# Opening loads split over two DMA queues, the first tile and the last output tile worked in halves

## The chip, the cores and the metric

The kernel runs on one core of one Trainium2 chip. The metric is device time in microseconds (us) of one execution; lower is better. A core has a matrix engine (TensorE, PE in the profile), a vector engine (VectorE, DVE), a scalar engine (ScalarE, ACT), GpSimd (POOL) and SyncE (SP), which here only issues DMA transfers. Each works through its own list of instructions in order and waits on semaphores for the others. The DMA engines, 16 for the core, move data between DRAM and the on-chip memory; a queue of requests can belong to SP or to ACT. PSUM, where PE writes its results, has eight banks of 128 x 512 float32.

## The reference

The input x has 2048 rows (tokens) of 1024 columns. Two kinds of layer alternate, A, B, A, B, each added to x after a norm of every row:

```python
x = x + _A_ref(_layernorm(x), A_wqkv, A_wo)
x = x + _B_ref(_layernorm(x), B_w_gate, B_w_up, B_w_down)
# and the same two again
# _A_ref, 32 heads of 32 columns, with phi(t) = where(t > 0, t + 1, exp(t)) + 1e-6:
q, k, v = split(x @ wqkv)
kv, z = sum_s phi(k)[s] v[s]^T, sum_s phi(k)[s]
out = (phi(q) @ kv) / (phi(q) . z + 1e-6) @ wo
# _B_ref:
out = ((x @ w_gate) * (x @ w_up)) @ w_down
```

The values are bfloat16. The four norms all run over complete rows, so nothing of a tile can be normed before all its 1024 columns are there.

## The kernel before

The tokens are cut into 16 tiles of 128 rows, four tiles to a group. The tensor X holds all of them on the chip from beginning to end. The instructions of each engine stand in the order in which the code emits them; nothing is reordered, and the code places work of other engines between matmuls through small plans (`at(step, ...)`, `mid`). Buffers are taken from and returned to lists in turn (`slots` for 128 x 4096 buffers, `banks` for PSUM).

**Start.** All loads go through SP's queue in one file: tiles x0 and x1 (`load_x`, L93, 256 KB each), the first slab of key weights in two transfers (`load_cols` with `parts=2`, L99, 512 KB each: the first holds the weight rows for k = 0 to 3, the second those for k = 4 to 7), x2, x3, the second key slab (1 MB), x4, a value slab, and so on. A slab is the 1024 x 512 block of `wqkv` that makes 512 output columns. ACT begins with a load of its function table (L103). Transfers use eight semaphores in turn, so from the ninth on a request waits until the transfer eight before it has landed.

Meanwhile PE runs 11 matmuls on a zeroed buffer (`warm_up`, L125). For tile 0, `ln_stats` (L234, two halves of 512 columns, and L237) takes mean and variance on DVE, `ln_norm` computes the reciprocal deviation on ACT (L258, L260) and writes the normed tile `xn` on DVE (L262), and `tr_tile` has PE transpose it in eight 128 x 128 blocks into one PSUM bank (L279), which ACT copies out in two halves (L280, L281). Four more warm-up matmuls stand behind the transposes. The first group alone is transposed in this way; later groups are transposed by DMA requests in SP's list (L274).

Then `kv_eight` makes keys and values in chunks of one tile by 512 columns, eight matmuls over k to a chunk (L642). The first four chunks are (tile 0, slab 0), (tile 1, slab 0), (tile 0, slab 1), (tile 1, slab 1). The work for tiles 1, 2 and 3 is emitted between the matmuls of these chunks:

```python
order[0:4] = [(0, 0), (1, 0), (0, 1), (1, 1)]
mid.update({(0, 0, 5): ((tr_tile, 0, 1), (ln_norm, 0, 2), (ln_stats, 0, 3, (1,))),
            (1, 0, 5): ((ln_norm, 0, 3),),
            (0, 1, 3): ((tr_tile, 0, 2),), (1, 1, 3): ((tr_tile, 0, 3),)})
```

So the first chunk's six matmuls for k = 0 to 5 are followed by tile 1's transposes, then by k = 6 and 7.

**End.** The last step of the last layer (`down_seven` with `final`, i = 4) adds a product of 14 matmuls (L1182) to the PSUM bank of each of four tiles. For tiles 0 to 3 in turn: 14 matmuls of 128 x 512, then `after` has DVE scale the bank, add X and write X (`read`, L1155), and `finish` requests the store of that 128 x 512 block to `out` from SP (L1065, 128 KB).

Of the kernel before, what the change touches and what calls it, by code (L numbers as in the profile page):

```python
# [10 lines left out]
ALU = mybir.AluOpType  # L11
AX = mybir.AxisListType
BF16 = mybir.dt.bfloat16
# [22 lines left out]
def kernel(  # L36
# [11 lines left out]
    nc = tc.nc  # L48
    P = 128
    S, D = A_x.shape[1], A_x.shape[2]  # L50
    F = B_w_gate.shape[1]
    NT = S // P
    KD = D // P
    KH = KD // 2
# [3 lines left out]
    TPG = G // P  # L58
    NB = 512
    DC = D // NB  # L60
    NQD = KF // 2
    WPC = 7
# [10 lines left out]
    x_view = A_x[0].rearrange("(t p) d -> p t d", p=P)  # L73
    o_view = out[0].rearrange("(t p) d -> p t d", p=P)
    wqkv_v = A_wqkv.rearrange("(k p) n -> p k n", p=P)
# [5 lines left out]
    X = const.tile([P, NT, D], BF16, tag="X", name="X")  # L81
    slots = Free([const.tile([P, 4096], BF16, tag=f"s{i}", name=f"s{i}") for i in range(17)])
    temps = Free([const.tile([P, NB], F32, tag=f"f{i}", name=f"f{i}") for i in range(12)])
    banks = Free([psum.tile([P, NB], F32, tag=f"b{i}", name=f"b{i}") for i in range(8)])

    def v3(s, n):
        return s[:].rearrange("p (k n) -> p k n", n=n)

    def h3(s, n):
        return s[:].bitcast(F16).rearrange("p (k n) -> p k n", n=n)  # L90

    def load_x(t):
        nc.sync.dma_start(out=X[:, t, :], in_=x_view[:, t, :])  # L93

    def load_cols(view, n, parts=1):
        s = slots.get()
        w = KD // parts
        for r in range(parts):
            nc.sync.dma_start(out=v3(s, NB)[:, r * w:(r + 1) * w, :],  # L99
                              in_=view[:, r * w:(r + 1) * w, n * NB:(n + 1) * NB])  # L100
        return s

    nc.scalar.preload_act_table_set("natural_log_exp_and_others")  # L103
    wA = {}
    load_x(0)
    load_x(1)
    wA["k"] = [load_cols(wqkv_v, DC, 2)]
    load_x(2)
    load_x(3)
    wA["k"].append(load_cols(wqkv_v, DC + 1))  # L110
    load_x(4)
    wA["v"] = [load_cols(wqkv_v, 2 * DC)]
    load_x(5)
    load_x(6)
# [8 lines left out]
    def warm_up(n):  # L123
        for _ in range(n):
            nc.tensor.matmul(out=warmb[:], lhsT=warm[:].bitcast(BF16)[:, 0:P], rhs=warm[:].bitcast(BF16)[:, 0:NB],  # L125
                             start=True, stop=True)

    warm_up(11)
    ident = const.tile([P, P], BF16, tag="ident", name="ident")
# [121 lines left out]
        nc.scalar.activation(out=xn[:], in_=X[:, t, :], func=ACT.Identity, bias=nmr[:], scale=rstd[:])  # L251
        lns[(li, t)] = xn

    def ln_norm(li, t):
        mv = lns[(li, t)]
        half = li % 2 == 1
        rstd = small.tile([P, 1], F32, tag="rstd", name="rstd")
        nc.scalar.activation(out=rstd[:], in_=mv[:, 1:2], func=ACT.Ln, bias=(eps5x if half else eps5)[:],  # L258
                             scale=1.0 / (XS * XS) if half else 1.0)
        nc.scalar.activation(out=rstd[:], in_=rstd[:], func=ACT.Exp, scale=-0.5)  # L260
        xn = xnp.tile([P, D], F16 if li else BF16, tag="xn", name="xn")
        nc.vector.tensor_scalar(out=xn[:], in0=X[:, t, :], scalar1=mv[:, 0:1], scalar2=rstd[:],  # L262
                                op0=ALU.subtract, op1=ALU.mult)
        lns[(li, t)] = xn

    def tr_tile(li, t):
        xn = lns.pop((li, t))
        g, tl = divmod(t, TPG)
        if (li, g) not in xnTs:
            xnTs[(li, g)] = slots.get()  # L270
        s = xnTs[(li, g)]
        xnT = (h3 if li else v3)(s, NB)
        if (li, g) != (0, 0):
            nc.sync.dma_start_transpose(out=xnT[:, :, tl * P:(tl + 1) * P], in_=xn[:])  # L274
            return
        b = banks.get()
        pt = b[:].bitcast(BF16).rearrange("p (k n) -> p k n", n=P)
        for k in range(KD):
            nc.tensor.transpose(out=pt[:, k, :], in_=xn[:, k * P:(k + 1) * P], identity=ident[:])  # L279
        nc.scalar.copy(out=xnT[:, 0:KH, tl * P:(tl + 1) * P], in_=pt[:, 0:KH])  # L280
        nc.scalar.copy(out=xnT[:, KH:KD, tl * P:(tl + 1) * P], in_=pt[:, KH:KD])  # L281
        banks.put(b)

    def phi_exp(b, c):
        m = temps.get()
# [205 lines left out]
    def kv_seven(kvp):  # L491
# [5 lines left out]
        for t, i in zip(range(2 * TPG, NT), (3, 8, 17, 31, 36, 45, 59, 64)):  # L497
            at(i, ln_stats, 2, t, (0,))
            if i % 14 == 8:
                at(i + 5, ln_norm, 2, t)  # L500
                at(i + 6, tr_tile, 2, t)
            else:
                at(i + 4, ln_rstd, 2, t)
                at(i + 6, ln_apply, 2, t)
                at(i + 7, tr_tile, 2, t)
# [367 lines left out]
    def ffn_pass(li, p, W):  # L873
        q = li - 1 + p
        xs = [xnTs.pop((li, 2 * p + g)) for g in range(2)] + xqs.pop((li, p))
        x0, x1, ta, tb = (h3(s, NB) for s in xs)
        mv = [x0[:, 0:KH], x0[:, KH:KD], x1[:, KH:KD], tb[:, KH:KD], ta[:, 0:KH], ta[:, KH:KD], tb[:, 0:KH]]
        st = [0, 1, 7, 3, 4, 5, 6]
        hs = []
        wd = []  # L880
# [177 lines left out]
        def xrow(g, tl, n):  # L1058
            t = (2 * p + g) * TPG + tl
            return t, X[:, t, n * NB:(n + 1) * NB], o_view[:, t, n * NB:(n + 1) * NB]  # L1060

        def finish(g, tl, n):
            _, o, d = xrow(g, tl, n)
            if li == 3:
                nc.sync.dma_start(out=d, in_=o)  # L1065

        nl = (li, 1) if p == 0 else (li + 1, 0)
        W2 = Weights(q + 1)
# [3 lines left out]
    def down_seven(q, li, p, hs, wd, load_piece, cast_piece, ORDER, at, run, finish, xrow, nl, W2, final):  # L1072
        sg = [slots.get(), slots.get()]

        def blocks(r):
            v = []
            for a in range(2):
                h, pos = hpos(a, 2 * r)
                v.append(h3(hs[h], 2 * G)[:, pos:pos + 2, :])
            return [v[a][:, :, g * G:(g + 1) * G] for g in range(2) for a in range(2)]  # L1080

        def sview(r):
            return h3(sg[r // 4], G)[:, 2 * (r % 4):2 * (r % 4) + 2, :]
# [10 lines left out]
        def lhs(i, j, tl):  # L1094
            if i in (1, 2, 4):
                v = blocks(j // 2)[{1: 0, 2: 1, 4: 3}[i]][:, j % 2, :]
            else:
                v = sview(j // 2)[:, j % 2, :]
            return v[:, tl * P:(tl + 1) * P]
# [9 lines left out]
        if nl[0] < 4:  # L1109
            for u in range(2 * TPG):  # L1110
                t = nl[1] * 2 * TPG + u
                i = 2 + 7 * u if p == 0 or u < TPG else 56 + 9 * (u - TPG)
# [37 lines left out]
        bank = {}  # L1150
        u = {}

        def read(o, g, tl, n, src, keep=None):
            _, x, _ = xrow(g, tl, n)
            nc.vector.scalar_tensor_tensor(out=o, in0=src, scalar=kap[:], in1=x if keep is None else keep,  # L1155
                                           op0=ALU.mult, op1=ALU.add)

        def after(i, tl):
            b = bank[("a" if i in (1, 6, 7, 4) else "c" if i in (5, 3) else "b", tl)]
            if i in (1, 5, 6):  # L1160
                g, n = {1: (0, 0), 5: (1, 1), 6: (0, 1)}[i]
                u[(i, tl)] = temps.get()
                read(u[(i, tl)][:], g, tl, n, b[:])
                return
            g, n, k = {3: (0, 1, 6), 7: (1, 1, 5), 2: (0, 0, 1), 4: (1, 0, None)}[i]
            t = u.pop((k, tl)) if k else None
            _, x, _ = xrow(g, tl, n)
            read(x, g, tl, n, b[:], t[:] if k else None)
            if k:
                temps.put(t)  # L1170
            if i in (3, 2, 4):
                banks.put(b)
            finish(g, tl, n)

        for pi, i in enumerate(ORDER):
            if i in (1, 5, 2):
                for tl in range(TPG):
                    bank[({1: "a", 5: "c", 2: "b"}[i], tl)] = banks.get()
            key = "a" if i in (1, 6, 7, 4) else "c" if i in (5, 3) else "b"

            def mm(j, tl):
                nc.tensor.matmul(out=bank[(key, tl)][:], lhsT=lhs(i, j, tl),  # L1182
                                 rhs=h3(wd[2 * pi + j // WPC], NB)[:, j % WPC, :],
                                 start=(j == 0 and i in (1, 5, 2)), stop=(j == NQD - 1), skip_group_check=True)

            if final and i == 4:
                for tl in range(TPG):
                    for j in range(NQD):
                        mm(j, tl)
                    after(i, tl)  # L1190
                continue
            for j in range(NQD):
                for tl in range(TPG):
                    mm(j, tl)
                if j % WPC == WPC - 1:
                    slots.put(wd[2 * pi + j // WPC])
                    load_piece()
                if i == 7 and j == 7:
                    slots.put(sg[0])
                if i == 7 and j == NQD - 1:  # L1200
                    slots.put(sg[1])
                if i == 4 and j % 4 == 1:
                    slots.put(hs[j // 4 * 2])
                run(pi * NQD + j)
            for tl in range(TPG):
                after(i, tl)
# [24 lines left out]

    ln_stats(0, 0)
    ln_stats(0, 1, (0,))
    ln_norm(0, 0)
    tr_tile(0, 0)
    ln_stats(0, 1, (1,))
    ln_norm(0, 1)
    ln_stats(0, 2)
    ln_stats(0, 3, (0,))
    warm_up(4)  # L1240
    temps.put(warm)
    banks.put(warmb)
    for li in (0, 2):
# [33 lines left out]
```

## Time and profile before

| | |
|---|---|
| median of 3 runs | 1498.24 us (1497.96 to 1499.23) |
| profiled execution | 1497.85 us |
| its span, first to last instruction | 1496.1 us |
| PE busy | 1489.2 us, 7109 matmuls |
| DVE / ACT / POOL busy | 985.5 / 811.0 / 89.4 us |
| moved by DMA | 253.90 MB, mean 170 GB/s |

The profile is of one execution. A row of the timeline gives the start and the length in us, the engine, the line of the code, the operation, what is written and read with shapes, how often (x), and in brackets how long the engine idled before and what released it. SPq stands for requests that SP issues; their length is that of issuing, and the views of DMA issues give the time from issue to landing. The chain of waits follows the program back from its last instruction, at each step to what released it. Matmul rows overlap: one of 512 columns is shown some 0.38 us long, but the next starts 0.216 later.

### The profile page before, as it was taken

The numbers are of one execution on the slowest core, as the hardware profiler recorded it, in microseconds if no ns is written. First come the engines' busy times: TensorE is split into PE (matmuls) and PEld (weight loads), VectorE is DVE, ScalarE is ACT, GpSimd is POOL, SyncE is SP. The second block draws the span as 40 slices with busy tenths as digits, with TensorE's granted clock in tenths as the row PEclk, the third lists the DMA queues.
The fourth block names the chain that finished last, engine by engine and source line by source line (L and its number), as shares of the span: only waits on it lengthen the run. The fifth ranks groups of instructions, "written<-read, shape, count | busy, mean of one in ns | idle before, by whom it ended". The sixth has DMA issues, their size and how long they took to land.

```text
span 1496.1 us, 18380 instructions
## 1 busy us (share of the span) xinstructions
PE 1489.2 (100%) x7109; PEld 683.0 (46%) x7109; DVE 985.5 (66%) x1659; ACT 811.0 (54%) x1185; POOL 89.4 (6%) x46
## 2 busy tenths in 40 slices
PE   9999999999999999999999999999999999999999
PEld 4454444444444444444444444444444444444444
DVE  6667989988677666657877686854445844444452
ACT  4678875777558477764557675623335213333420
POOL 0000004962000000000000000000000000000000
PEclk9999999999999999999999999999999999999999
DMA  7696146465469788758531101464332787343613
GB/s 246 174 304 232 57 91 201 132 211 155 131 201 313 256 260 261 250 210 254 179 85 27 37 29 49 114 235 166 136 126 94 190 271 315 113 169 114 212 58 130
DMA packets 219655, 253.90 MB, mean 170 GB/s; under 512 B 68528, under 2 KB 195504, under 8 KB 208816
## 3 DMA queue, kind: packets, MB, share of 16 engines
q1 hardware_dynamic: 219568, 252.74, 53.3%
q8 instruction: 55, 0.90, 0.2%
q14 instruction: 32, 0.26, 0.1%
HBM read 196.08 MB, written 40.89 MB: 158 GB/s over the span
## 4 chain that ended last, share of the span: by engine, by line
PE 97%; DVE 2%; DMA 1%; ACT 0%; SPq 0%; issue 0%; DVEq 0%; ACTq 0%
PE b L942 45%; PE b L1182 23%; PE b L642 7%; PE b L779 7%; PE b L810 7%; PE b L571 6%; PE b L793 1%; DMA s<-in_A_wqkv_dram 1%; PE b L661 1%; PE b L760 0%; PE b L525 0%; DVE st L234 0%; DVE X L1155 0%; ACT f L287 0%; DVE X L812 0%; DVE s L293 0%
## 5 line engine op out<-in xcount | busy, mean ns | idle before, releaser
L942 PE MATMUL b<-s,s 128*128 128x512 f16 x3136 | 677.7, 379 | 0.0
L942 PEld LDWEIGHTS <-s 128*128 128x128 f16 x3136 | 306.7, 98 | 369.9
L1182 PE MATMUL b<-s,s 128*128 128x512 f16 x1568 | 339.1, 379 | 0.0
L958 DVE TENSOR_TENSOR f<-f,b 128x512 f32<-128x512 f32 x232 | 159.3, 687 | 223.7 <-ACT f L947 209.5
L947 ACT COPY f<-b 128x512 f32<-128x512 f32 x284 | 166.0, 584 | 224.6 <-PE b L942 224.6
L1182 PEld LDWEIGHTS <-s 128*128 128x128 f16 x1568 | 153.3, 98 | 185.1
L953 ACT COPY b<-b 128x512 f32<-128x512 f32 x104 | 59.3, 570 | 128.4 <-PE b L942 128.4
L444 ACT ACTIVATE s<-s,scw 128x1024 f16<-128x1024 bf16 x112 | 122.7, 1151 | 2.0 <-DMA s<-in_B_w_gate_dram 1.8
L779 PE MATMUL b<-s,s 128*128 128x512 bf16 (+1 forms) x512 | 120.3, 379 | 0.0
L810 PE MATMUL b<-s,s 128*128 128x512 bf16 x512 | 118.5, 379 | 0.3 <-DVE s L802 0.3
L908 ACT ACTIVATE s<-s,scw 128x1792 f16<-128x1792 bf16 x48 | 83.0, 1783 | 61.2 <-DMA s<-in_B_w_down_dram 56.6
L642 PE MATMUL b<-s,s 128*128 128x512 bf16 x512 | 112.0, 379 | 0.6 <-DMA s<-in_A_wqkv_dram 0.4
L863 POOL TENSOR_SCALAR s<-s,scw 128x1024 f16<-128x1024 bf16 x28 | 87.8, 3151 | 257.2 <-DMA s<-in_B_w_down_dram 243.8
L962 DVE SCALAR_TENSOR_TENSOR s<-f,b 128x512 f16<-128x512 f32 x108 | 74.2, 687 | 40.9 <-PE b L942 24.6
L571 PE MATMUL b<-s,s 128*128 128x512 f16 x448 | 98.3, 379 | 0.2
L962 DVE SCALAR_TENSOR_TENSOR s<-f,f 128x512 f16<-128x512 f32 x116 | 83.3, 718 | 4.0
L810 PEld LDWEIGHTS <-s 128*128 128x128 bf16 x512 | 50.0, 98 | 60.9 <-DVE s L802 1.0
L642 PEld LDWEIGHTS <-s 128*128 128x128 bf16 x512 | 49.7, 98 | 60.1 <-ACT s L280 1.0
L779 PEld LDWEIGHTS <-s 128*128 128x128 bf16 (+1 forms) x512 | 50.0, 98 | 59.4
L234 DVE BATCH_NORM_STATS2 st<-X 128x6 f32<-128x512 bf16 x112 | 71.7, 681 | 2.2 <-DMA X<-in_A_x_dram 2.2
L1090 DVE TENSOR_TENSOR s<-s,s 128x1024 f16<-128x1024 f16 x80 | 52.9, 678 | 23.3 <-PE b L1182 23.3
L571 PEld LDWEIGHTS <-s 128*128 128x128 f16 x448 | 43.5, 98 | 52.3 <-issue 1.2
(123 smaller groups left out, 1096.2 us busy)
## 6 DMA issues: line engine op xcount, KB each, us to landing
s<-wc SPq DMA_DIRECT2D x56, 1024.0 KB, 6.6
s<-dc SPq DMA_DIRECT2D x32, 896.0 KB, 5.7
wc<-s SPq DMA_DIRECT2D x28, 1024.0 KB, 5.2
s<-in_B_w_down_dram SPq DMA_DIRECT2D x24, 896.0 KB, 5.8
s<-in_A_wqkv_dram SPq DMA_DIRECT2D x17, 1024.0 KB, 8.0
s<-in_B_w_down_dram SPq DMA_DIRECT2D x14, 1024.0 KB, 8.2
s<-in_B_w_gate_dram SPq DMA_DIRECT2D x28, 512.0 KB, 6.7
s<-in_B_w_up_dram SPq DMA_DIRECT2D x28, 512.0 KB, 7.8
```

The costliest lines, as they stand in the source:

```text
L444: nc.scalar.activation(out=h, in_=v, func=ACT.Copy, scale=scw[:, m:m + 1])
L571: nc.tensor.matmul(out=b[:], lhsT=lhs[i][:, k, pr * P:(pr + 1) * P], rhs=rhs[:, k, :], start=k == 0 and (i in (1, 5) or i == 2 and w == "v ...
L642: nc.tensor.matmul(out=b[:], lhsT=xnT[:, k, tl * P:(tl + 1) * P], rhs=w[:, k, :], start=(k == 0), stop=(k == KD - 1))
L779: nc.tensor.matmul(out=b[:], lhsT=w[:, k, j * P:(j + 1) * P], rhs=xnT[:, k, :], start=(k == 0), stop=(k == KD - 1))
L810: nc.tensor.matmul(out=b[:], lhsT=v3(pqs[g], G)[:, c, tl * P:(tl + 1) * P], rhs=v3(M[n], NB)[:, c, :], start=(c == 0), stop=(c == KD - 1))
L863: nc.gpsimd.tensor_scalar(out=h3(s, D)[:, i, :], in0=v3(s, D)[:, i, :], scalar1=scw[:, 2:3], scalar2=None, op0=ALU.mult)
L908: nc.scalar.activation(out=v.bitcast(F16)[:, r * w:(r + 1) * w], in_=v[:, r * w:(r + 1) * w], func=ACT.Copy, scale=scw[:, 2:3])
L942: nc.tensor.matmul(out=o[m][:], lhsT=W.get(j, m, st[i - 1], k), rhs=mv[i - 1][:, k, :], start=start and k == 0, stop=stop and k == KH - 1, ...
L947: nc.scalar.copy(out=d[m][:], in_=o[m][:])
L958: nc.vector.tensor_tensor(out=d[m][:], in0=d[m][:], in1=o[m][:], op=ALU.add)
L962: nc.vector.scalar_tensor_tensor(out=h3(hs[h], 2 * G)[:, pos, g * G:(g + 1) * G], in0=x[:], scalar=HS, in1=y[:], op0=ALU.mult, op1=ALU.mult)
L1182: nc.tensor.matmul(out=bank[(key, tl)][:], lhsT=lhs(i, j, tl), rhs=h3(wd[2 * pi + j // WPC], NB)[:, j % WPC, :], start=(j == 0 and i in (1 ...
```

## The change

`load_x` and `load_cols` take a list of queues and split their transfer among them: x0 and x1 in column halves, the first half from SP's queue and the second from ACT's; the first key slab's first half from ACT's queue and its second from SP's; x2 and x3 whole from ACT's. Everything behind stays in SP's list. For tile 0, `ln_norm` writes `xn` in two passes of 512 columns and `tr_tile` transposes into two banks, four blocks each, so that each copy on ACT has a bank of its own. Two warm-up matmuls are left of the four behind them. At the end, tile 3's 14 matmuls are done as two sets of 14 with 256 columns each, the first set before tile 2's matmuls and the second after them, each with its own read and its own store of 64 KB.

```diff
--- before.py
+++ after.py
@@ -89,24 +89,27 @@
     def h3(s, n):
         return s[:].bitcast(F16).rearrange("p (k n) -> p k n", n=n)
 
-    def load_x(t):
-        nc.sync.dma_start(out=X[:, t, :], in_=x_view[:, t, :])
-
-    def load_cols(view, n, parts=1):
+    def load_x(t, queues=(nc.sync,)):
+        w = D // len(queues)
+        for i, q in enumerate(queues):
+            q.dma_start(out=X[:, t, i * w:(i + 1) * w], in_=x_view[:, t, i * w:(i + 1) * w])
+
+    def load_cols(view, n, queues=(nc.sync,)):
         s = slots.get()
-        w = KD // parts
-        for r in range(parts):
-            nc.sync.dma_start(out=v3(s, NB)[:, r * w:(r + 1) * w, :],
+        w = KD // len(queues)
+        for r, q in enumerate(queues):
+            q.dma_start(out=v3(s, NB)[:, r * w:(r + 1) * w, :],
                               in_=view[:, r * w:(r + 1) * w, n * NB:(n + 1) * NB])
         return s
 
     nc.scalar.preload_act_table_set("natural_log_exp_and_others")
     wA = {}
-    load_x(0)
-    load_x(1)
-    wA["k"] = [load_cols(wqkv_v, DC, 2)]
-    load_x(2)
-    load_x(3)
+    both = (nc.sync, nc.scalar)
+    load_x(0, both)
+    load_x(1, both)
+    wA["k"] = [load_cols(wqkv_v, DC, both[::-1])]
+    load_x(2, both[1:])
+    load_x(3, both[1:])
     wA["k"].append(load_cols(wqkv_v, DC + 1))
     load_x(4)
     wA["v"] = [load_cols(wqkv_v, 2 * DC)]
@@ -251,7 +254,7 @@
         nc.scalar.activation(out=xn[:], in_=X[:, t, :], func=ACT.Identity, bias=nmr[:], scale=rstd[:])
         lns[(li, t)] = xn
 
-    def ln_norm(li, t):
+    def ln_norm(li, t, parts=1):
         mv = lns[(li, t)]
         half = li % 2 == 1
         rstd = small.tile([P, 1], F32, tag="rstd", name="rstd")
@@ -259,11 +262,13 @@
                              scale=1.0 / (XS * XS) if half else 1.0)
         nc.scalar.activation(out=rstd[:], in_=rstd[:], func=ACT.Exp, scale=-0.5)
         xn = xnp.tile([P, D], F16 if li else BF16, tag="xn", name="xn")
-        nc.vector.tensor_scalar(out=xn[:], in0=X[:, t, :], scalar1=mv[:, 0:1], scalar2=rstd[:],
-                                op0=ALU.subtract, op1=ALU.mult)
+        w = D // parts
+        for r in range(parts):
+            nc.vector.tensor_scalar(out=xn[:, r * w:(r + 1) * w], in0=X[:, t, r * w:(r + 1) * w], scalar1=mv[:, 0:1],
+                                    scalar2=rstd[:], op0=ALU.subtract, op1=ALU.mult)
         lns[(li, t)] = xn
 
-    def tr_tile(li, t):
+    def tr_tile(li, t, parts=1):
         xn = lns.pop((li, t))
         g, tl = divmod(t, TPG)
         if (li, g) not in xnTs:
@@ -273,13 +278,13 @@
         if (li, g) != (0, 0):
             nc.sync.dma_start_transpose(out=xnT[:, :, tl * P:(tl + 1) * P], in_=xn[:])
             return
-        b = banks.get()
-        pt = b[:].bitcast(BF16).rearrange("p (k n) -> p k n", n=P)
+        bs = [banks.get() for _ in range(parts)]
+        pts = [b[:].bitcast(BF16).rearrange("p (k n) -> p k n", n=P) for b in bs]
         for k in range(KD):
-            nc.tensor.transpose(out=pt[:, k, :], in_=xn[:, k * P:(k + 1) * P], identity=ident[:])
-        nc.scalar.copy(out=xnT[:, 0:KH, tl * P:(tl + 1) * P], in_=pt[:, 0:KH])
-        nc.scalar.copy(out=xnT[:, KH:KD, tl * P:(tl + 1) * P], in_=pt[:, KH:KD])
-        banks.put(b)
+            nc.tensor.transpose(out=pts[k * parts // KD][:, k, :], in_=xn[:, k * P:(k + 1) * P], identity=ident[:])
+        nc.scalar.copy(out=xnT[:, 0:KH, tl * P:(tl + 1) * P], in_=pts[0][:, 0:KH])
+        nc.scalar.copy(out=xnT[:, KH:KD, tl * P:(tl + 1) * P], in_=pts[-1][:, KH:KD])
+        banks.put(*bs)
 
     def phi_exp(b, c):
         m = temps.get()
@@ -1059,10 +1064,10 @@
             t = (2 * p + g) * TPG + tl
             return t, X[:, t, n * NB:(n + 1) * NB], o_view[:, t, n * NB:(n + 1) * NB]
 
-        def finish(g, tl, n):
+        def finish(g, tl, n, cols=slice(0, NB)):
             _, o, d = xrow(g, tl, n)
             if li == 3:
-                nc.sync.dma_start(out=d, in_=o)
+                nc.sync.dma_start(out=d[:, cols], in_=o[:, cols])
 
         nl = (li, 1) if p == 0 else (li + 1, 0)
         W2 = Weights(q + 1)
@@ -1178,16 +1183,23 @@
                     bank[({1: "a", 5: "c", 2: "b"}[i], tl)] = banks.get()
             key = "a" if i in (1, 6, 7, 4) else "c" if i in (5, 3) else "b"
 
-            def mm(j, tl):
-                nc.tensor.matmul(out=bank[(key, tl)][:], lhsT=lhs(i, j, tl),
-                                 rhs=h3(wd[2 * pi + j // WPC], NB)[:, j % WPC, :],
+            def mm(j, tl, cols=slice(0, NB)):
+                nc.tensor.matmul(out=bank[(key, tl)][:, cols], lhsT=lhs(i, j, tl),
+                                 rhs=h3(wd[2 * pi + j // WPC], NB)[:, j % WPC, cols],
                                  start=(j == 0 and i in (1, 5, 2)), stop=(j == NQD - 1), skip_group_check=True)
 
             if final and i == 4:
-                for tl in range(TPG):
+                half = NB // 2
+                for tl, cols in ((0, None), (1, None), (3, slice(0, half)), (2, None), (3, slice(half, NB))):
                     for j in range(NQD):
-                        mm(j, tl)
-                    after(i, tl)
+                        mm(j, tl, cols or slice(0, NB))
+                    if cols is None:
+                        after(i, tl)
+                        continue
+                    x = xrow(1, tl, 0)[1][:, cols]
+                    read(x, 1, tl, 0, bank[(key, tl)][:, cols], x)
+                    finish(1, tl, 0, cols)
+                banks.put(bank[(key, 3)])
                 continue
             for j in range(NQD):
                 for tl in range(TPG):
@@ -1231,13 +1243,13 @@
 
     ln_stats(0, 0)
     ln_stats(0, 1, (0,))
-    ln_norm(0, 0)
-    tr_tile(0, 0)
+    ln_norm(0, 0, 2)
+    tr_tile(0, 0, 2)
     ln_stats(0, 1, (1,))
     ln_norm(0, 1)
     ln_stats(0, 2)
     ln_stats(0, 3, (0,))
-    warm_up(4)
+    warm_up(2)
     temps.put(warm)
     banks.put(warmb)
     for li in (0, 2):
```

## Prediction

> **What bounds the kernel now.** I read the shares of the span first: PE is busy 1489.2 of 1496.1 us, so it idles about 7 us in all, and a change that adds no PE work can win back only what lies there. The chain of waits gives PE 97%. The table by stretches puts 2.6 us of PE idle before 14 us and 3.4 us behind the last matmul. The change touches these two places, so I read those alone. At the start the chain, in order of time, has these pieces:
>
> ```profile
> 3.76 8.98 DMA s<-in_A_wqkv_dram
> 12.74 0.04 issue
> 12.78 1.02 PE b L642 x4
> 13.81 0.45 PE b L279 x8
> 14.25 1.73 PE b L642 x8
> ```
>
> PE runs without a break from 12.78 on, and what releases it there is the second key slab (k1, 1 MB), requested at 3.76, landed at 12.74. Whatever the start gains is how far that 12.78 moves. The timeline has what lies ahead of it:
>
> ```profile
> 0.71 1.28 ACT L103 ACT_TABLE_LOAD   x1 [0.71 <-PEq L1261]
> 3.62 1.29 DVE L234 BATCH_NORM_STATS2 st<-X 128x6 f32<-128x512 bf16 x2 [2.24 <-DMA X<-in_A_x_dram]
> 5.81 0.55 DVE L262 TENSOR_SCALAR xn<-X,mv,rstd 128x1024 bf16<-128x1024 bf16 x1
> 6.41 0.62 PE L279 MATMUL b<-ident,xn 128*128 128x128 bf16 x8 [0.57 <-DVE xn L262]
> 7.07 0.58 ACT L280 COPY s<-b 128x512 bf16<-128x512 bf16 x1 [1.29 <-PE b L279]
> 7.73 1.46 PE L642 MATMUL b<-s,s 128*128 128x512 bf16 x6
> 9.21 0.62 PE L279 MATMUL b<-ident,xn 128*128 128x128 bf16 x8
> 10.50 1.90 PE L642 MATMUL b<-s,s 128*128 128x512 bf16 x8 [0.24 <-ACT s L280]
> ```
>
> This is a second chain beside the transfers: tile 0's norm, transposes, copy, six matmuls of the first chunk, tile 1's transposes, its copy, eight matmuls of the second chunk. At 0.216 us each (1.73 for eight) these eight end at 10.50 + 1.73 = 12.23. So had k1 been there, PE would have gone on at 12.23: the transfer costs 0.55, the rest is this chain. The table by stretches shows how full the DMA engines were (last columns: granted clock, DMA share, GB/s):
>
> ```profile
> 3.25:3.50 0.25, 0.25 (x2) 0.01 (x1) 0.00 (x0) 0.00 (x0) 0.00 (x0) 1.00 1.03 401
> 3.75:4.00 0.25, 0.25 (x2) 0.03 (x1) 0.25 (x1) 0.00 (x0) 0.00 (x0) 1.00 0.36 119
> 4.25:4.50 0.25, 0.25 (x2) 0.10 (x1) 0.25 (x2) 0.00 (x0) 0.00 (x0) 1.00 0.44 111
> 4.75:5.00 0.25, 0.25 (x2) 0.15 (x1) 0.22 (x2) 0.00 (x0) 0.00 (x0) 1.00 1.03 336
> ```
>
> Full up to 3.5, a pause of about 1.1 us at some 145 of 385 GB/s when the tiles x0 and x1 are through and the first key slab begins, full again from 4.75. The pause loses 1.1 x (1 - 145/385) = 0.7 us of transfer. At the end the timeline has
>
> ```profile
> 1480.75 13.07 SPq L1065 DMA_DIRECT2D out_dram<-X  x8
> 1492.71 0.75 DVE L1155 SCALAR_TENSOR_TENSOR X<-b,kap,X 128x512 bf16<-128x512 f32 x1 [2.27 <-PE b L1182]
> ```
>
> PE ends at 1492.68; then a read of 0.75, a store requested at 1493.49 that lands 1.7 later, and 0.9 to the end of the span. Those 3.4 us are in series.
>
> **The end, part by part.** The last output tile becomes two column halves, one before tile 2's and one after it. PE: 28 matmuls of 256 columns for 14 of 512. No row has 256; 128 columns (transposes) take 0.056, 512 take 0.216, so on the line between them 0.109: 28 x 0.109 - 14 x 0.216 = 0.03 longer (bounds 0 to 0.1). Only the second half's read is left behind the last matmul: 512 columns take 0.745, the nearest smaller form that reads PSUM with two scalars (128 columns, L738) 0.343, so 256 take some 0.48: 0.27 saved. The store is 64 KB for 128 KB: 256 KB stores land in 2.5, 128 KB in 1.7, so by that slope 64 KB gains 0.4; if all of the 1.7 is fixed, nothing. I take 0.2. The extra read (0.48), SP request (0.33) and store of the first half lie beside tile 2's 14 matmuls (3.0 us), and tile 2's own read (0.75) and request beside the 1.5 us of matmuls that follow it. Without that cover the first half's store would queue 0.33 ahead of the last. End: 0.27 + 0.2 - 0.03 = **0.44 saved** (0.2 to 0.65).
>
> **The start, part by part.** Norm in halves: a 512-wide pass of this kind takes 0.29 (L301), so PE gets the first half 0.55 - 0.29 = 0.26 earlier. Two banks: the first copy waits for four transposes, not eight, 0.45 / 2 = 0.22 earlier. Sum 0.48: first key matmul 7.73 to 7.25, and as ACT's copies move too, and tile 1's rstd sits behind them on ACT, its norm, its transposes and the second chunk also move by 0.48, whose end goes from 12.23 to 11.75. Two of four warm-up matmuls go (0.43); PE waits for the copy then, so they are worth nothing.
>
> Transfers. SP's list is now half of x0, half of x1, k's second half, k1; ACT's is the other halves, k's first half (k0a), x2, x3. SP issues a request in about 0.45, so k1 is asked for at 2.1 rather than 3.76, behind 0.75 MB of its own queue. ACT pays five requests, some 2.2 us; its next work is the rstd at 5.25, after 3.25 idle, so they are free if done by then. ACT's x3 waits for x0's first half (about 3.6), and behind that wait stands the rstd that everybody needs: 3.6 + 0.45 leaves 1.2 us. SP's x4 now waits for a half of x1; behind it are v slabs and tiles first read after 19 us, and transposes at 22.98, all with slack. Splitting x0 gains me nothing: the later half decides, and both come at about 3.6 (by the store slope 0.4 sooner at best; 1.3 later in the second rival).
>
> The price is k0a. It used to be third in a single file, at 1.64 + 5.3 = 6.94, ready before its matmul. Now both halves of the slab travel side by side and arrive together, when 1.5 MB has come; in the run before, that was k0b at 2.11 + 6.3 = 8.4. If the pause goes, since a second queue has work while the first is slow to start, it is 8.4 - 0.7 = 7.7. From k0a's landing L to the next chunk it is 6 x 0.216 + (10.50 - 9.21) + 8 x 0.216 = 4.32, so 12.02. k1, the last of 3 MB, likewise 12.74 - 0.7 = 12.04. Both ends meet near 12.04: **0.74 saved at the start** (bounds: 1.03 gained with k0a by 7.25, 0.8 lost, below). Nothing between start and end changes order on any engine, and PE waits on nothing else for over a microsecond, so the shift should last to the end.
>
> Sum: 0.74 + 0.44 = 1.18. The profiled execution took 1497.85 (span 1496.1 and 1.75 around it), 0.39 under the median of 1498.24. So 1496.67 in its terms, **1497.1** as a median: 0.08% faster.
>
> **Rivals.** (1) *The transfers are the bound anyway.* From 4.75 to k1's landing the engines' share is 0.93 to 1.12; two queues can't fill what is full. If the pause belongs to the first slab's rows and not to its queue, it comes again, k1 lands at 12.74 and k0a at up to 8.4 (8.4 + 4.32 = 12.72). The start gives nothing, the end 0.44: 1497.4, median 1497.8. Against it: 0.36 share in the pause is an engine with room. The Trainium skill, page "DMA: Bandwidth & Descriptors", section "Issuing engines are not separate DMA queues", says this of all such splits: requests from several engines run on the same 16 DMA engines, and only issue time is saved. By that rule the answer is this rival's; from 4.75 on the trace agrees, in the pause it can't tell.
>
> (2) *ACT's requests stand behind its table load: slower.* ACT's list begins with the table load (0.71 to 1.99). If a request waits for it, x0's second half is asked for at 2.0 and k0a at 2.0 + 2 x 0.45 = 2.9, while SP's queue has the engines to itself. With the 5.3 and 6.3 of the slab's halves k0a lands at 8.2 to 9.2. It decides from L = 12.78 + 0.44 - 4.32 = 8.9 on: above, more is lost than the end gives. At 9.2: 13.52, 0.74 lost, 0.30 slower net: 1498.15, median 1498.5. No row has a request on ACT, so nothing speaks for or against. The Trainium skill, page "Advanced Engine Details and Errata", section "Sequencer and Instruction Queues", has the sequencer push engine instructions into a queue and read on, by which the request would not wait; no run here shows it.
>
> (3) *All goes well.* k0a by 7.25, k1 by 11.75: 1.03 + 0.65 = 1.68, 1496.2, median 1496.6.
>
> **Numbers.** Forecast 0.40, rival 1 0.20, rival 2 0.17, rival 3 0.07; 0.16 for what this profile can't hold: a second queue's cost in or around the span, or a TensorE that falls back to the pace of its first 11 matmuls (0.427 each) while it waits longer with fewer warm-ups, some 2 us (the granted clock reads 1.00 even there, so the trace would not name it). A measurement of this kernel tells 0.2%, 3 us, from no change. All four cases lie inside; of the rest I give 0.06 to faster and 0.10 to slower by more. Runs before lay 0.3 below to 1.0 above their median: the range goes from rival 3 less the wider of these, 1495.6, to rival 2 with it added, 1499.5.
>
> **What would show it.** Right: k1 landing near 12, PE unbroken from there, no low share between 3.5 and 4.75, first key matmul released by k0a near 7.7, last read 0.48. Rival 1: the pause again. Rival 2: ACT's first request after 1.99, first key matmul after 8.5. Wrong: PE idle beyond 14 us that was not there, matmuls 0.427 apart after the transposes, or a larger gap between span and time.

## The result and the profile after

The changed kernel is slower: 1500.73 us median of 22 runs (1497.57 to 1502.86) against 1498.21 (1497.44 to 1499.47) for the kernel before, a ratio of 1.0014 with a 95% interval of 1.0008 to 1.0021. The 22 runs form two groups. Eight have a mean granted clock of 1.000 and a median of 1498.67, fourteen have 0.998 or 0.999 and a median of 1501.20. The profiled execution of the changed kernel, 1498.65 with a span of 1496.6, is of the first group. The difference from before must therefore be read twice: what the profile shows, and what it does not show because it is of the first group.

The timeline of the changed kernel, to be laid beside the one of before:

```profile
0.71 1.28 ACT L105 ACT_TABLE_LOAD   x1 [0.71 <-PEq L1273]
0.74 0.88 ACTq L95 DMA_DIRECT2D X<-in_A_x_dram  x2
5.70 0.73 DVE L267 TENSOR_SCALAR xn<-X,mv,rstd 128x512 bf16<-128x512 bf16 x2
6.17 0.72 PE L284 MATMUL b<-ident,xn 128*128 128x128 bf16 x8
6.63 0.58 ACT L285 COPY s<-b 128x512 bf16<-128x512 bf16 x1 [0.97 <-PE b L284]
6.72 0.59 PE L128 MATMUL b<-f 128*128 128x512 bf16 x2
9.08 1.46 PE L647 MATMUL b<-s,s 128*128 128x512 bf16 x6 [1.76 <-DMA s<-in_A_wqkv_dram]
11.66 2.76 PE L647 MATMUL b<-s,s 128*128 128x512 bf16 x12 [0.25 <-ACT s L285]
```

ACT's requests (ACTq) go out at 0.74, beside the table load. The copy of tile 0 starts at 6.63 instead of 7.07. And then PE waits 1.76 us for the first half of the key slab: the first key matmul is at 9.08, where it was at 7.73. The eight matmuls of the second chunk, now the first of the row at 11.66, end at 11.66 + 1.73 = 13.39, and PE goes straight on to the second key slab; that point was 12.78 before. So the start is 0.61 later. The views of DMA issues give size and time from issue to landing of the two halves, both requested at 1.65:

```profile
s<-in_A_wqkv_dram SPq DMA_DIRECT2D x1, 512.0 KB, 5.0
s<-in_A_wqkv_dram ACTq DMA_DIRECT2D x1, 512.0 KB, 7.4
```

The half that is needed second came at 6.7, the half that is needed first at 9.04. The second key slab (requested at 2.1, 10.0 to landing) was there at 12.1, before PE was ready for it. In the table by stretches the pause of before is gone. The first line is before, the second after (the last two figures are DMA share and GB/s):

```profile
3.50:4.75 1.25, 1.25 (x4) 0.44 (x3) 1.13 (x2) 0.00 (x0) 0.00 (x0) 1.00 0.53 153
3.50:4.75 1.25, 1.25 (x4) 0.45 (x3) 1.25 (x2) 0.00 (x0) 0.00 (x0) 1.00 1.09 384
```

At the end the timeline of the changed kernel has

```profile
1493.57 0.48 DVE L1160 SCALAR_TENSOR_TENSOR X<-b,kap,X 128x256 bf16<-128x256 f32 x1 [0.78 <-PE b L1187]
```

From this read to the end of the span are 1496.6 - 1493.57 = 3.03 us, before 1496.1 - 1492.71 = 3.39. From the read of tile 0 to the last one it is 9.10 instead of 9.07. The end gives 0.33. The read of tile 0 itself comes 0.83 later than before, where the start is 0.61 later: some 0.2 comes in between, and its cause is open.

### The profile page after: what moved, and what is told of

Same layout as the page of the kernel before. It is cut to its first block, busy times and chain, and to the rows that moved or that the text cites. A ratio compares the mean times of both kernels' runs of the same rounds, so it can differ in the third digit from the quotient of the medians.

```text
span 1496.6 us, 18377 instructions
## 1 busy us (share of the span) xinstructions
PE 1487.4 (99%) x7088; PEld 684.4 (46%) x7121; DVE 986.0 (66%) x1661; ACT 810.7 (54%) x1185; POOL 88.9 (6%) x46
## 4 chain that ended last, share of the span: by engine, by line
PE 95%; DVE 2%; DMA 2%; ACT 1%; issue 0%; SPq 0%; ACTq 0%; DVEq 0%
PE b L947 45%; PE b L1187 21%; PE b L647 7%; PE b L784 7%; PE b L815 7%; PE b L576 6%; DMA s<-in_A_wqkv_dram 1%; PE b L798 1%; PE b L666 1%; DMA s<-dc 0%; PE b L765 0%; PE b L530 0%; DVE st L237 0%; ACT f L292 0%; DVE X L1160 0%
## 5 line engine op out<-in xcount | busy, mean ns | idle before, releaser
L947 PE MATMUL b<-s,s 128*128 128x512 f16 x3136 | 677.7, 379 | 0.0
L1187 PE MATMUL b<-s,s 128*128 128x512 f16 (+1 forms) x1582 | 339.3, 377 | 0.1
L576 PE MATMUL b<-s,s 128*128 128x512 f16 x448 | 98.3, 379 | 0.2
```

The source lines that it names most:

```text
L576: nc.tensor.matmul(out=b[:], lhsT=lhs[i][:, k, pr * P:(pr + 1) * P], rhs=rhs[:, k, :], start=k == 0 and (i in (1, 5) or i == 2 and w == "v ...
L947: nc.tensor.matmul(out=o[m][:], lhsT=W.get(j, m, st[i - 1], k), rhs=mv[i - 1][:, k, :], start=start and k == 0, stop=stop and k == KH - 1, ...
L1187: nc.tensor.matmul(out=bank[(key, tl)][:, cols], lhsT=lhs(i, j, tl), rhs=h3(wd[2 * pi + j // WPC], NB)[:, j % WPC, cols], start=(j == 0 an ...
```

## The experiments

There are two theories. Theory 1: two queues bring the first key slab late, PE idles for it, and in most executions the idle PE falls back to half its pace, which costs more than the waiting itself. Theory 2: all of it is transfers, and the slower group is the one whose slab is later still. Pace is the spacing of the matmuls, 0.216 us for 512 columns at a granted clock of 1.00 and about 0.43 at 0.50. Each kernel had 11 runs, and is compared with runs of the kernel before on the same chip.

**The changed kernel again.** No edit.

> The changed kernel itself, once more. Its 22 runs fall in two groups: seven near 1498.6 with a mean granted clock of 1.000 and fifteen near 1501 with 0.998 to 1.000; the profile of after is of the first group. Theory 1 (pace): the first key slab's first half, on ACT's queue, lands at 9.04 in place of 6.94, PE idles from 7.3 to 9.08, and in most executions TensorE has fallen back to the pace of its first matmuls by then, which costs 2 to 2.5 us more. Theory 2 (transfers): the slower runs are those in which that half lands 2 us later still. A profile of the slower group shows by theory 1 the half landing near 9.0 as before and key matmuls some 0.43 apart for about 3 to 5 us behind it; by theory 2 the first key matmul near 11 and all of them 0.216 apart. Times by both: 1498.5 to 1502, two groups.

Measured: 1500.32 median, ratio 1.0015 (1.0006 to 1.0024). Three runs with a clock of 1.000 (median 1498.36), eight below (1500.97). None of the 33 runs of before beside it was below 1.000. The profile was again of the first group, so it does not tell the theories apart:

```profile
9.13 1.46 PE L647 MATMUL b<-s,s 128*128 128x512 bf16 x6 [1.40 <-DMA s<-in_A_wqkv_dram]
```

The first half was as late as in the first profile. The rest of the transfers was not the same: the second key slab landed at 2.1 + 10.9 = 13.0 instead of 12.1, and the stretch from 3.50 to 4.75 had 311 GB/s instead of 384.

**Eleven warm-up matmuls.**

```diff
-    warm_up(2)
+    warm_up(11)
```

> The changed kernel with 11 instead of 2 warm-up matmuls behind tile 0's transposes: from 6.7 on they take 11 x 0.216 = 2.4 us, up to about 9.1, where the first half of the key slab lands. No transfer and no wait is changed. Theory 1 (pace): PE no longer idles, the slower group is gone, all runs near 1498.7 with a clock of 1.000, so 2 us faster than the changed kernel's median. Theory 2 (transfers): no effect, two groups, median near 1500.7.

Measured: 1499.36, ratio 1.0008 (0.9999 to 1.0017), all 11 runs at a clock of 1.000. Its profile, the timeline:

```profile
6.65 2.54 PE L128 MATMUL b<-f 128*128 128x512 bf16 x11
10.57 1.46 PE L647 MATMUL b<-s,s 128*128 128x512 bf16 x6 [1.38 <-DMA s<-in_A_wqkv_dram]
```

In this execution the slab was still later (10.57), and PE idled 1.38 us, yet neither this run nor the ten others fell to the lower clock. The slower group is gone, as theory 1 has it, and theory 2, by which all of it is transfers, is out. The mean went from 1500.42 to 1499.29 on the same chip: 1.1 of the 2.3 over before (mean 1498.14). The other 1.1 stays, more than the 0.6 expected: with the pace kept, something still costs, and the late slab is the only wait that this profile shows.

**The end alone.** The kernel before with the column halves of the last tile.

```diff
-                for tl in range(TPG):
+                for tl, cols in ((0, None), (1, None), (3, slice(0, half)), (2, None), (3, slice(half, NB))):
...
```

> The kernel before with the last output tile in column halves and nothing else. From the last read to the end of the span the two profiles have 3.39 (before) and 3.03 (after), and 28 narrow matmuls for 14 cost 0.03 more, so both theories expect 0.33 us less than before, near 1497.9, in one group. A third theory, that the end costs something that the one profile of after does not show, expects no gain or a loss.

Measured: 1498.43 against 1498.12, ratio 1.0001 (0.9993 to 1.0010). The expected 1497.9 did not come, and an interval of 1 us or more to either side can't tell a third of a microsecond from the third theory. The traces can: from the last read to the end of the span it is 2.9 to 3.05 us in eight profiles of kernels with the column halves, and 3.4 in the two without them. (A ninth with halves, of the next experiment, has 4.65: there the last store took 3.1 us to land, in all others 1.5.) One of the 11 runs, at 1499.01, had a mean clock of 0.999; in the profile the clock falls at 1495.9, behind the last matmul, where it costs nothing, and such a fall lowers the mean too. Which of the two falls that run had is not known.

This profile also has the loads of before, and there the first half landed at 1.64 + 6.0 = 7.7, and PE waited for the second key slab:

```profile
13.50 1.02 PE L647 MATMUL b<-s,s 128*128 128x512 bf16 x4 [0.75 <-DMA s<-in_A_wqkv_dram]
```

The 6.9 and 12.78 of the profile that the prediction was made from were a good draw. The 13.39 of the changed kernel's profile is not later than this 13.50, so the 0.61 by which its start is behind lies within what one kernel does from one execution to the next. What lies beyond it is the first half of the slab: in four profiles with one file in the order of before, or with only the second slab moved up, it landed at 6.3 to 7.7, in five with it on ACT's queue at 9.0 to 10.5.

**Both halves of the slab on SP's queue.** x0 and x1 stay split, x2 and x3 stay on ACT's.

```diff
-    wA["k"] = [load_cols(wqkv_v, DC, both[::-1])]
+    wA["k"] = [load_cols(wqkv_v, DC, (nc.sync, nc.sync))]
```

> The changed kernel with both halves of the first key slab on SP's queue, first half first (x0 and x1 still split over both queues, x2 and x3 on ACT's). The first half takes the place that the second half had in the changed kernel, landing near 6.7; the second half near 8. First key matmul near 7.3, second key slab near 12, PE unbroken from about 12.0 in place of 13.4. Both theories expect one group near 1497.0 (0.7 to 1.0 us from the start, 0.33 from the end). If two groups are seen here without the long idle of PE, theory 1 falls.

Measured: 1499.69, ratio 1.0010 (1.0001 to 1.0019); six runs at 1.000 (median 1498.59), five below (1500.79). My expectation of one group near 1497.0 failed: the first half landed at 1.64 + 7.5 = 9.2. x2 and x3 on the other queue went through beside it (x2 was there at 7.8), and the pause was there again in part (240 GB/s from 3.50 to 4.75). So it is not ACT's queue that is slow; what is requested on a second queue takes its share from what is needed first. This profile is of the slower group, and the timeline and the table by stretches name what happens (the third figure from the end is the granted clock):

```profile
9.22 2.67 PE L647 MATMUL b<-s,s 128*128 128x512 bf16 x6 [1.98 <-DMA s<-in_A_wqkv_dram]
```
```profile
9.20:9.30 0.10, 0.08 (x1) 0.08 (x1) 0.10 (x2) 0.00 (x0) 0.00 (x0) 1.00 1.13 399
9.30:9.40 0.10, 0.10 (x1) 0.01 (x1) 0.10 (x1) 0.00 (x0) 0.00 (x0) 0.53 1.07 379
9.50:12.50 3.00, 3.00 (x14) 1.58 (x13) 1.06 (x3) 0.00 (x0) 0.00 (x0) 0.50 1.09 358
12.70:12.80 0.10, 0.10 (x2) 0.00 (x0) 0.00 (x0) 0.02 (x1) 0.00 (x0) 0.91 1.06 358
```

PE had idled since about 7.2; its first key matmul was at 9.22, and at 9.3 the clock fell to half, until 12.7.

**All loads in one file again**, the rest of the change kept.

```diff
-    load_x(0, both)
+    load_x(0)
... (x1, x2, x3 likewise; both halves of the slab on nc.sync)
```

> The changed kernel with all loads back in SP's single file as before; the halves of the first tile, the two warm-up matmuls and the column halves at the end stay. Theory 1 (two queues make the key slab late, the late slab makes PE idle, the idle PE slows down): the slab's first half lands at 6.9 to 7.6 again, PE idles under 1 us ahead of it, no run with a clock of 0.999 or less, one group. The halves gain up to 0.5 where the transfers allow it, the end 0.33: 1497.3 to 1498.1. A rival, that the halves of the first tile and the two missing warm-up matmuls cost the time, expects the slower group here too and a median over 1499.5.

Measured: 1498.00 against 1498.24, ratio 1.0000 (0.9991 to 1.0009), all at a clock of 1.000, the shortest span of all profiles (1495.8). The halves and the missing warm-ups do no harm by themselves. They do no good that the times show either, and the timeline shows why:

```profile
7.23 1.04 PE L647 MATMUL b<-s,s 128*128 128x512 bf16 x4
8.55 0.59 PE L647 MATMUL b<-s,s 128*128 128x512 bf16 x2 [0.29 <-DMA s<-in_A_wqkv_dram]
12.92 1.02 PE L647 MATMUL b<-s,s 128*128 128x512 bf16 x4 [0.75 <-DMA s<-in_A_wqkv_dram]
```

The first key matmul is at 7.23, 0.5 earlier as reckoned. Then PE waits for the slab's second half, and at 12.92 for the second slab: what the halves win is handed back to the transfers.

**The loads alone.** The kernel before with the two-queue loads only, four warm-up matmuls.

> The kernel before with the two-queue loads and nothing else of the change (one norm pass, one bank, four warm-up matmuls, whole last tile). Theory 1: the slab's first half lands at 9 to 10.5 as in the changed kernel; PE's idle is shorter by the two more warm-up matmuls and the later transposes, some 1.1 instead of 1.9 us, so a share of the runs still falls to the slower pace, fewer than in the changed kernel; median 1499.3 to 1500.8, slower than before by 1 to 2.5. The rival (halves and warm-ups cost the time) expects no more than 0.7 over before.

Measured: 1498.57, ratio 1.0003 (0.9995 to 1.0012), all 11 at a clock of 1.000. In its profile the slab was as late, but with later transposes and two more warm-ups PE idled less:

```profile
9.08 1.46 PE L647 MATMUL b<-s,s 128*128 128x512 bf16 x6 [1.05 <-DMA s<-in_A_wqkv_dram]
```

No run fell, where I expected a share of them to, and the median is under what I expected; taken alone, this is what the rival forecast. The kernel with all loads in one file refutes the rival: the halves and the two missing warm-ups cost nothing either, and neither part alone makes the slower group. It takes both, the late slab and the work of PE that ends earlier ahead of it. The mean here is 0.55 over before; the load split costs about half a microsecond while the pace holds, though the interval includes no change.

**The idle in one queue.** The changed kernel with all loads on SP's, the first key slab behind x2, x3 and x4.

> The changed kernel with all loads on SP's queue, but the first key slab behind x2, x3 and x4 (0.75 MB more ahead of it), so that its first half lands near 9 with no second queue at work. Theory 1: as PE idles from 7.3 to about 9 here too, the two groups come back, with clocks of 0.998 to 0.999 in the slower, 1 to 2 us over the same kernel with the slab in its old place. If it is not the idle time but the second queue that slows TensorE, there is one group here with a clock of 1.000.

Measured: 1500.02, ratio 1.0012 (1.0003 to 1.0021); three runs at 1.000 (median 1498.52), eight below (1500.18). Timeline and stretches of its profile:

```profile
9.11 2.66 PE L647 MATMUL b<-s,s 128*128 128x512 bf16 x6 [1.71 <-DMA s<-in_A_wqkv_dram]
11.56 1.06 PE L284 MATMUL b<-ident,xn 128*128 128x128 bf16 x8
```
```profile
9.20:9.30 0.10, 0.10 (x1) 0.01 (x1) 0.10 (x2) 0.00 (x0) 0.00 (x0) 0.52 1.05 369
12.60:12.70 0.10, 0.10 (x2) 0.00 (x0) 0.00 (x0) 0.04 (x1) 0.00 (x0) 0.92 1.10 348
```

Six key matmuls take 2.66 instead of 1.46, eight transposes 1.06 instead of 0.61. No second queue is at work here, so the fall does not need one. With the eleven warm-up matmuls, which keep the late slab and fill the wait, it is the idle time that slows TensorE. The groups lie 1.7 us apart here.

**Four warm-up matmuls.** The changed kernel with `warm_up(4)`.

> The changed kernel with the four warm-up matmuls of before behind tile 0's transposes in place of two. Nothing else differs, so the first key slab still lands near 9. PE's idle ahead of it is some 0.4 shorter than in the changed kernel (about 1.3 where its profile shows 1.76), between that and the 1.05 of the kernel with the loads alone, where no run of 11 fell below a clock of 1.000 (22 of 33 of the changed kernel's did). Theory 1 expects clearly fewer runs below 1.000, 0 to 4 of 11, and a median of 1498.5 to 1499.3: the two removed matmuls are then what turns 0.5 us of loss into 2. If 6 to 8 of 11 fall, the missing warm-ups are not what decides, but the earlier transposes or the load itself.

Measured: 1499.38, ratio 1.0012 (1.0003 to 1.0021), three of 11 runs below 1.000, with the changed kernel 22 of 33. The count is as theory 1 has it, the median just above what I expected. In its profile, of a run at a clock of 1.000, the slab came at 9.5, so PE idled as long as in the profile above that fell:

```profile
9.50 1.46 PE L647 MATMUL b<-s,s 128*128 128x512 bf16 x6 [1.72 <-DMA s<-in_A_wqkv_dram]
```

The removed warm-ups matter, but two do not cover a slab that comes late by more than they last. And the length of the idle time alone does not decide whether the clock falls; the last section has more on this.

**The second slab ahead of x2 and x3**, in one file, the transposes of tiles 2 and 3 one chunk later.

> A version that might beat both: loads in SP's single file, the second key slab ahead of x2 and x3 (it lands 0.5 MB or 1.4 us earlier, near 11.4 to 12), the transposes of tiles 2 and 3 one chunk later each so that they find their tiles, the halves and the end as in the changed kernel. By theory 1 PE does not idle long before the first key matmul (about 7.3) and need not wait for the second slab: unbroken from 11.8 to 12.3 in place of 12.78, and the end 0.33 less: 1497.2, one group, 0.9 less than before. If tiles 2 and 3, which then land at 12.0 and 12.7, come too late, PE waits before the fifth chunk and the gain is lost.

Measured: 1498.98, ratio 1.0007 (0.9998 to 1.0016), one run of 11 (1499.66) at a clock of 0.999. The wait moved: PE did not stop for the second slab, and then stood before tile 2's keys:

```profile
10.27 4.49 PE L647 MATMUL b<-s,s 128*128 128x512 bf16 x19 [0.25 <-ACT s L285]
17.71 1.04 PE L647 MATMUL b<-s,s 128*128 128x512 bf16 x4 [1.37 <-ACT s L285]
```

The case named at the end of the expectation came about, and the version does not beat the one before. The kernel that came nearest to beating both was the one in a single file, within a thousandth of the kernel before.

## Why the prediction was wrong

I forecast 1497.1, 0.08% faster; it is 0.14% slower and outside the range (1499.5 at its upper end).

**Right.** The end: the read of 256 columns took 0.48 as reckoned, the last store landed in 1.5 instead of 1.7, PE paid 0.03; 0.33 in the changed kernel's profile against a term of 0.44. The halves of the first tile moved the copy by 0.44 and, in one file, the first key matmul to 7.23 (7.25 forecast).

**Right by luck.** The pause went in the profile after, and the second key slab landed at 12.1 (12.04 forecast). The second queue did not do this. The same stretch, 3.50 to 4.75, of the same kernel again and of the loads alone, both with two queues, has

```profile
3.50:4.75 1.25, 1.25 (x4) 0.45 (x3) 1.04 (x2) 0.00 (x0) 0.00 (x0) 1.00 0.92 311
3.50:4.75 1.25, 1.25 (x4) 0.44 (x3) 1.22 (x2) 0.00 (x0) 0.00 (x0) 1.00 0.89 197
```

and the kernels with one file had 153 to 294 GB/s there. The second slab landed at 13.0 in the changed kernel's other profile.

**Wrong, the term that failed: the price of k0a.** The step was that both halves of the slab arrive together when 1.5 MB has come, at 7.7. The first came at 9.04. By the table by stretches 2.23 MB had moved by 8.5 us (1.5 us at 269 GB/s, 1.25 at 384, 1.75 at 352, 1.5 at 362, 0.5 at 375), where the two tiles and the slab are 1.57 million bytes. The rest, some 0.7 MB, was k1, x2 and x3, and when the first half landed SP's queue had moved 1.22 MB and ACT's 1.21, together 0.86 MB more than the tiles and the slab. In the single file of before these transfers stood behind the slab, and only 1.96 MB had moved when all of it was there at 8.38. The 0.47 MB between 1.96 and 2.43, at the 362 GB/s of that time, are 1.3 us: the way from 7.7 to 9.04. In two queues SP's file had run on to k1 while ACT's was still on k0a. I counted who shares with k0a inside the slab and left out what both queues had behind it. So the 0.74 saved became 0.61 lost in this profile, and what k1 won was taken from the transfer that PE needed first.

**Wrong, the second step: "Two of four warm-up matmuls go (0.43); PE waits for the copy then, so they are worth nothing."** They are worth nothing while the slab is there at 7.2. With the slab at 9, PE idles 1.4 to 2 us, and in 22 of 33 runs the clock was below 1.000. I had the price of this nearly right (2 us; in the one-queue kernel's profile the second chunk starts at 13.30 and ends at 15.03, where the same first matmul at full pace gives 9.11 + 4.32 = 13.43, so 1.6), but put it among the unexplained 0.16 instead of where it belongs: it hangs on the lateness of k0a, so it should have been in the second rival, which has k0a at 8.2 to 9.2. That rival would then have ended at 1498.5 + 1.6 = 1500.1, near the median. I also wrote that the trace would not name it; it does, with a granted clock of 0.50.

**The rivals.** The second had the landing (9.04, above its deciding point of 8.9) and the sign, by a mechanism that is refuted: ACT's first request went out at 0.74, during the table load. With that, what the Trainium skill says in "Advanced Engine Details and Errata", section "Sequencer and Instruction Queues", agrees with the trace. The first rival had it right that two queues can't fill what is full: the same engines served both queues, about 350 to 390 GB/s once running, whoever asked, and what changed was the order. The page "DMA: Bandwidth & Descriptors" of the Trainium skill, section "Issuing engines are not separate DMA queues", which has all requests run on the same 16 DMA engines, agrees with that. The rival's own signs, k1 at 12.74 and k0a at up to 8.4, did not come, and it forecast no loss. The pause is no matter of queues: at 3.50 to 4.75 it is weaker or stronger from one execution to the next.

**Not settled.** The two groups of the changed kernel lie 2.5 apart, the fall of pace measures 1.6 in two profiles of its relatives. Executions with a later slab idle longer and should fall more often, which would add to the difference; no profile of the changed kernel itself in the slower group was caught, so this is argued, not shown. Two things fit it. In the one-queue kernel the groups lie only 1.7 apart, the fall alone; and eight falls in 11 runs at 1.6 each make 1.2 of the mean, where eleven warm-up matmuls took away 1.1. Part can be something else: in the profile with both halves on SP's queue 1.6 of what it has over the others lies in its last store. Why eleven warm-up matmuls leave a mean of 1.1 over before, and the loads alone 0.55, is not explained. Why SP's half of the slab came 2.4 us ahead of ACT's in one profile and 0.4 ahead in another is open too.

## What to carry to other kernels

Before a load is spread over a second queue, list everything that is requested behind the first transfer that somebody waits for: in one file it waits its turn, in two files it takes a share of the same engines. A wait put in front of TensorE costs its length and, at 1.7 us or so in this kernel, the chance of a stretch at half pace; matmuls on dummy data that last until about the time when the data is there kept all 11 runs at full pace here, and removing such matmuls is only free as long as nothing ahead of them is late. A profile is one draw: if the times of a kernel fall in groups, look at the mean granted clock of each run before explaining the one execution that was profiled, and then at where in a trace the clock falls, since a fall behind the last matmul lowers the mean too.

## What the runs showed of the hardware

The clock stood at half for the same length in both profiles that caught it: from 9.31 to 12.72 and from 9.20 to 12.62, 3.41 us (from the 0.1 us stretches in which it changed), though the waits, the loads and the queues differed. The Trainium skill, page "TensorE: Matmul & The Clock Gate", section "Part 1: The HAM clock gate (the "warmup" mystery)", has activity judged in free-running windows of 3413 ns. The length agrees with it, and so does that the same kernel falls in some executions and not in others. The page also says that the clock falls after an idle window of about 3.4 us; here PE idled 1.7 to 2.0 us ahead of the fall, so a window that is idle throughout is not needed. Of the kernel whose profile shows 1.05 us of idle none of 11 runs fell.

The length of the idle time does not settle it: 1.71 us fell, 1.72 and 1.76 did not. What differs in these traces is when the clock had first risen. Their clock records begin with full pace, at 5.89 and 5.79 us in the two that fell, and the fall comes just 3.41 later. In these 3.41 us the table by stretches has PE busy for 1.43 and 1.57; in the same length from the rise on it has 1.66 in the changed kernel's profile (rise at 6.27, 1.76 idle), 1.99 with four warm-up matmuls (5.62, 1.72 idle) and 2.0 or more in all other profiles whose rise is recorded. By these traces the start of full pace, which lay anywhere from 4.1 to 7.2 us, would place the window in which idle time counts. This fits, but it rests on two falls alone.

Such a table of granted clock misses the start of the kernel: it reads 1.00 in the first 5 us, where matmuls are 0.427 apart.
